# Gated linear recurrence and a cosine-gated MLP on one core: another written-out order of the same steps, with 65 in place of 78 changes of form on TensorE

## The chip, the cores and the metric

The kernel runs on one core of a Trainium2 chip. The metric is the device time of one execution in microseconds, the median of three runs. TensorE (PE in the profile; its weight loads are PEld), VectorE (DVE), ScalarE (ACT), GpSimd (POOL) and the DMA queues, which SyncE (SP) and GpSimd issue, each work through their own instructions in the order in which the kernel emits them.

## The reference

Two layers, one behind the other, in f32. The first is a recurrence over 768 steps for 4 batches and 8 heads of size 48, with a decay per step and channel:

```
state = alpha[:, :, t, :, None] * state + k[t] (outer) v[t]
y[t]  = q[t] @ state
```

The second takes x, the outputs of all heads side by side (3072 tokens x 384), through an MLP with 2048 hidden channels:

```
h = x @ w_in
g = h * cos(h)
out = g @ w_out
```

## The kernel before

Time is cut into pairs J = 0 to 11: three for each batch, each of 256 steps, which are two chunks of 128 in time. In a load, a partition holds two neighbouring steps (e = 0, 1), and the 128 partitions are two halves (c = 0, 1). The recurrence is done with cumulated logarithms, so that all of it is products:

- `load` (SP): alpha ("a"), k, q and v of a pair, 384 KB each. `w1` and `w2` (POOL): the MLP's weights, cast on the way. The load of alpha of pair 3 waits for the last product of yT of pair 1 (GATES, L99); all later loads stand behind it on SP.
- `ln` (ACT) takes logarithms; `mula` (POOL, pairs 3 and up) first multiplies the two steps of a partition. `cums0` and `cums` (PE) sum the logarithms over time by a product with a triangle, and over a chunk by a product with `inchunk`; `sub` (DVE) gives the sums for e = 0 of pairs 3 and up.
- `icp` and `exps` (ACT): exp of the sums, with minus and plus; `eb` is a session of both for a pair, with `ln` of the next. Exp and Sin need different tables, so ACT loads a table (L137, L366) where it goes from one to the other.
- `sk`, `sq` (POOL or DVE): k and q times these; `castv` (POOL): v to bf16; `vpe` and `vev` (PE and ACT or DVE), or `vst` (SP, DMAs), put v of a chunk in another layout. `decay` (POOL): the decay of a chunk.
- `trans` (PE, L259) turns k and q; `evT` (ACT or DVE, L265) takes them to SBUF. `scores` (PE, L273): q k for each chunk c, `mask` (DVE, L278) makes it causal. `outer` (PE, L290): k v of a chunk; `add` (DVE) and `state` (POOL) carry the state from chunk to chunk.
- `yT` (PE, L339): state by q plus scores by v, 32 columns of the array at a time; `evy` (ACT or DVE, L350): to the MLP's input `xT`.
- `m1` u.J (PE, L360): a quarter u of the hidden channels, 12 products; `sin` (ACT, L366), `gate` (DVE, L371); `m2` c p.J (PE, L389 and, for the very last half, L383): part p of the second product for chunk c, 4 products; `evo` (ACT or DVE, L401, L397) and `out` (SP): the result to HBM.
- `idle` n (PE, L415): n products of zeros, 128x512, into a PSUM tile that nobody reads.

Products are full where they use 128 rows and 128 columns of the array: L156, L168, L360, L389, L383, L415. They are partial with 64 rows (L259, L273, L290), with 64 rows and 64 columns (L235), and with 32 columns (L339).

PSUM: tag "h" has three slots of two banks, which `cums0`, `trans`, `scores`, `outer`, `yT` and `m1` share in the order of their emission; tags "x" and "o" have one bank each (`cums` and `vpe`; `m2` and `idle`). A step that takes a slot waits for the last reader of what was in it.

The order is written out: PLAN gives each step of each pair a number, and a letter where the engine is chosen (A for ACT, D for DVE); IDLE gives the products of zeros. The steps are emitted in the order of these numbers, and each engine's queue follows from that. No scheduler moves anything:

```
with tc.manual_schedule():
    for _, _, kind, args in sorted(order, key=lambda x: x[:2]):
        steps[kind](*args)
```

Of the kernel before, what the change touches and what calls it, by code (L numbers as in the profile page):

```python
# [16 lines left out]
def kernel(  # L17
# [11 lines left out]
    B, H, S, D = q.shape  # L29
# [64 lines left out]
    w1 = [consts.tile([C, KT, DF // 2], BF, tag=f"w1{r}", name="w1") for r in range(2)]  # L94
    w2 = consts.tile([C, NF, DM], BF, tag="w2", name="w2")
# [315 lines left out]
    def idle(n):  # L411
# [134 lines left out]
```

## Time and profile before

| what | value |
|---|---|
| time, median of 3 runs | 183.84 us (183.51 to 183.93) |
| profiled execution: span from the first to the last instruction | 182.3 us |
| PE busy | 175.4 us, 96% of the span, 2467 products |
| PEld / DVE / ACT / POOL busy | 132.6 / 134.8 / 129.9 / 71.4 us |
| DMA | 29.47 MB, 162 GB/s in the mean |
| `m2` products (L389) | 368, 67.1 us busy |
| `m1` products (L360) | 576, 67.0 us busy |
| products of zeros (L415) | 38 in the records, 11.1 us busy |

The span covers the program's own instructions; the time of a run has some start and end around it, 1.5 us here. Busy time of PE overlaps between products, since one starts before the one ahead of it has left the array: the time from one start to the next is what a product costs in a row of them. DMA queues are read by when the first user of a load goes on.

### The profile page before, as it was taken

The page shows a single profiled execution, that of the slowest core. Times are in us where ns is not written, and L with a number is a line of the kernel's source. Part 1 is how long each engine was busy: PE and PEld are TensorE (multiplying, and loading weights), DVE is VectorE, ACT ScalarE, POOL GpSimd, SP SyncE. Part 2 cuts the span into 40 slices and gives each one's busy share as a digit, 9 for nine tenths or more (in the row PEclk, how much of TensorE's full clock was granted, in tenths as well). Part 3 has the DMA queues.
Part 4 walks back from the last instruction along what each step waited for, and adds up shares of the span by engine and source line. Part 5 has one row for each costly group of instructions (what it writes and reads, how often), then busy time and mean ns, then how long its engine had stood idle before and what let it go on. Part 6 is the DMA issues. An engine that isn't in the chain of part 4 may idle for free.

```text
span 182.3 us, 5756 instructions
## 1 busy us (share of the span) xinstructions
PE 175.4 (96%) x2467; PEld 132.6 (73%) x2470; DVE 134.8 (74%) x183; ACT 129.9 (71%) x169; POOL 71.4 (39%) x104
## 2 busy tenths in 40 slices
PE   7999899989999999998999999999999999999993
PEld 2455789746697877975799669686876796787872
DVE  7188878678879897599889886978688778363460
ACT  2837687998989999959578999838964174383331
POOL 5145830377777103734894298240720320100000
PEclk9999999999999999999999999999999999999999
DMA  5999999999989959996629905690052142010032
GB/s 148 261 261 220 199 215 221 273 260 265 248 184 283 249 132 295 289 277 202 147 63 229 273 18 166 155 233 0 4 110 83 45 109 81 4 43 4 0 129 86
DMA packets 57801, 29.47 MB, mean 162 GB/s; under 512 B 50992, under 2 KB 56496, under 8 KB 57776
## 3 DMA queue, kind: packets, MB, share of 16 engines
q1 hardware_dynamic: 56256, 25.86, 58.3%
q0 software_dynamic: 1376, 3.15, 9.3%
q8 instruction: 19, 0.31, 0.7%
q10 hardware_dynamic: 144, 0.10, 0.2%
q14 instruction: 6, 0.05, 0.1%
HBM read 25.17 MB, written 4.72 MB: 164 GB/s over the span
## 4 chain that ended last, share of the span: by engine, by line
PE 77%; ACT 11%; DVE 6%; DMA 2%; issue 2%; ACTq 0%
PE h_ps L360 29%; PE o_ps L389 28%; PE y_ps L339 5%; DVE gsb L371 5%; PE idle_ps L415 4%; ACT c_sb L366 3%; PE A_ps L273 3%; PE T_ps L259 3%; DMA a<-in_alpha_dram 2%; PE U_ps L290 2%; ACT L366 2%; PE o_last L383 1%; ACT L137 1%; ACT lna L142 1%; PE cums_h L156 1%
## 5 line engine op out<-in xcount | busy, mean ns | idle before, releaser
L371 DVE TENSOR_TENSOR gsb<-h_ps,c_sb 128x1024 bf16<-128x1024 f32 x48 | 58.2, 1222 | 20.8 <-ACT c_sb L366 19.4
L366 ACT ACTIVATE c_sb<-h_ps,halfpi 128x1024 bf16<-128x1024 f32 x48 | 53.3, 1115 | 26.7 <-PE h_ps L360 26.4
L389 PE MATMUL o_ps<-w,gsb 128*128 128x384 bf16 x368 | 67.1, 327 | 0.6 <-DVE o_sb L401 0.6
L360 PE MATMUL h_ps<-xT,w 128*128 128x256 bf16 x576 | 67.0, 273 | 0.3 <-issue 0.2
L360 PEld LDWEIGHTS <-w 128*128 128x128 bf16 x576 | 62.4, 114 | 2.5 <-DMA w<-in_moe_w_in_dram 0.3
L389 PEld LDWEIGHTS <-gsb 128*128 128x128 bf16 x368 | 33.9, 98 | 21.4 <-issue 1.1
L312 POOL TENSOR_TENSOR un<-us,c 128x384 bf16<-128x384 f32 x20 | 16.8, 838 | 46.2 <-DVE us L304 36.9
L278 DVE TENSOR_TENSOR A_sb<-A_ps,msk 128x1024 bf16<-128x1024 f32 x24 | 28.9, 1216 | 3.4 <-PE A_ps L273 3.4
L217 POOL TENSOR_TENSOR qh<-q,cp 128x384 bf16<-128x384 f32 x13 | 13.8, 1063 | 13.3 <-ACT cp L201 12.2
L213 POOL TENSOR_TENSOR kh<-k,icp 128x384 bf16<-128x384 f32 x15 | 14.9, 1007 | 2.4 <-ACT icp L193 1.0
L220 POOL CAST vp<-v 128x768 bf16<-128x768 f32 x12 | 9.9, 827 | 12.0 <-DMA v<-in_v_dram 12.0
L150 POOL TENSOR_TENSOR a<-a 128x384 f32<-128x384 f32 x9 | 9.0, 1003 | 10.1 <-DMA a<-in_alpha_dram 10.1
L142 ACT ACTIVATE lna<-a 128x768 bf16<-128x768 f32 x12 | 10.1, 844 | 3.5 <-DMA a<-in_alpha_dram 3.3
L415 PE MATMUL idle_ps<-zeros 128*128 128x512 bf16 x38 | 11.1, 439 | 1.4 <-DVE halfpi L77 1.2
L401 ACT COPY o_sb<-o_ps 128x384 f32<-128x384 f32 x13 | 6.2, 478 | 8.5 <-PE o_ps L389 8.5
L137 ACT ACT_TABLE_LOAD x9 | 11.5, 1283 | 0.9 <-PEq L530 0.7
L366 ACT ACT_TABLE_LOAD x9 | 11.5, 1283 | 0.2
L304 DVE TENSOR_TENSOR us<-U_ps,un 128x384 f32<-128x384 f32 x16 | 8.8, 551 | 3.8 <-POOL un L312 2.1
L265 ACT COPY qkT<-T_ps 128x1024 bf16<-128x1024 bf16 x10 | 9.8, 1016 | 1.9 <-PE T_ps L259 1.8
L217 DVE TENSOR_TENSOR qh<-q,cp 128x384 bf16<-128x384 f32 x11 | 6.8, 629 | 5.4 <-DMA q<-in_q_dram 5.3
L265 DVE COPY qkT<-T_ps 128x1024 bf16<-128x1024 bf16 x14 | 9.4, 680 | 1.2 <-PE T_ps L259 1.2
L273 PE MATMUL A_ps<-qkT 48*128 48x128 bf16 x192 | 9.0, 217 | 0.7 <-DVE gsb L371 0.5
(70 smaller groups left out, 156.6 us busy)
## 6 DMA issues: line engine op xcount, KB each, us to landing
a<-in_alpha_dram SPq DMA_DIRECT2D x12, 384.0 KB, 5.9
q<-in_q_dram SPq DMA_DIRECT2D x12, 384.0 KB, 6.1
k<-in_k_dram SPq DMA_DIRECT2D x12, 384.0 KB, 6.0
v<-in_v_dram SPq DMA_DIRECT2D x12, 384.0 KB, 6.3
out_dram<-o_sb SPq DMA_DIRECT2D x23, 192.0 KB, 3.5
vs<-vp SPq DMA_DIRECT2D x36, 64.0 KB, 2.8
w<-in_moe_w_in_dram POOLq DMA_DIRECT2D x2, 768.0 KB, 9.6
w<-in_moe_w_out_dram POOLq DMA_DIRECT2D x4, 384.0 KB, 8.7
```

The costliest lines, as they stand in the source:

```text
L137: nc.scalar.preload_act_table_set("natural_log_exp_and_others")
L213: eng.tensor_tensor(out=kh_t[J % NQ][:, e, :, 0:D], in0=kqv["k", J][:, :, e], in1=icp_, op=ALU.mult)
L217: eng.tensor_tensor(out=qh_t[J % NQ][:, e, :, 0:D], in0=kqv["q", J][:, :, e], in1=cp, op=ALU.mult)
L265: copy(out=qkT_sb[J][:, c], in_=T_ps[J][:, c].rearrange("r n e s -> r n (e s)"))
L273: nc.tensor.matmul(A_ps[J, c][:, a, p, :], qkT[r, c, NP + p, :], qkT[r, c, p, :], start=True, stop=True)
L278: nc.vector.tensor_tensor(out=A_sb[J][:, c].rearrange("s a p t -> s (a p) t"), in0=A_ps.pop((J, c)).rearrange("s a p t -> s (a p) t"), in1 ...
L312: nc.gpsimd.tensor_tensor(out=u, in0=U_sum.pop(n), in1=c2_sb[J][:, :, c].unsqueeze(3).to_broadcast([C, NP, 2, D]), op=ALU.mult)
L360: nc.tensor.matmul(h_ps[J, u][:, f, :], cols, xT[J][:, kk, :], start=(kk == 0), stop=(kk == KT - 1))
L366: nc.scalar.activation(out=c_sb[J, u], in_=h_ps[J, u], func=AF.Sin, bias=halfpi, scale=1.0)
L371: nc.vector.tensor_tensor(out=gsb[J][:, u * FW : (u + 1) * FW], in0=h_ps.pop((J, u)), in1=c_sb.pop((J, u)), op=ALU.mult)
L389: nc.tensor.matmul(o_ps[J, c][:, 0:DM], gsb[J][:, ft, c * C : (c + 1) * C], w2[:, ft], start=(ft == 0), stop=(ft == NF - 1))
L415: nc.tensor.matmul(idle_ps[0], zeros[:, 0:C], zeros, start=True, stop=True)
```

## The change

The numbers in PLAN and IDLE are others; nothing else is edited, and every step of the computation is still done once. The new numbers only count up, in tens, where the old ones looked like nanoseconds; only their order has a meaning in both. What becomes different:

- the order of steps on every engine and on the queues of SP and POOL, from the first load on (alpha of pair 2, then 0 and 1, in place of 0 and 1);
- which of ACT, DVE and POOL does some of the steps: ACT has 10 `evy` in place of 14, 9 `evT` in place of 10, 4 `vev` in place of 5, 15 `evo` of a whole tile in place of 13; DVE has the others; DVE has 8 `sk` and 13 `sq` in place of 9 and 11, POOL the others;
- ACT changes its table 16 times in place of 18;
- on PE, neighbouring products have another form 65 times in place of 78;
- 30 products of zeros in place of 41.

The core of the diff:

```
     PLAN = {
-        "load a": "750 2205 4425 24496 25066 37693 43693 45193 55293 56793 62293 70470",
...
-        "cums0": "5565 7065 13604 - - - - - - - - -",
-        "cums": "5885 11199 13924 36668 44122 49975 61282 73275 86251 91443 105424 117024",
...
-        "icp 1": "8805 11929 15424 - - - - - - - - -",
...
-        "trans": "10624 16461 40648 44533 57020 68793 81884 90868 108663 115899 126133 137709",
-        "evT 0": "11929 17161:A 42626:A 45233:A 60041 70290:A 83189 93123 109551 117529:A 130540:A 139589",
-        "evT 1": "11324 18286 41348 46163:A 58511 71220:A 82584 91568 110631 116599:A 131821 138409:A",
...
-        "mask 0": "16671 19211 46257 47397 69298 74270 86411 102140 116819 126133 144562 152310",
...
-        "m1 1": "20895 30767 50275 64218 73575 93061 91743 120688 129985 146523 158739 168897",
...
+        "load a": "20 70 10 1150 1240 1670 1970 2060 2740 3160 2320 4240",
...
+        "cums0": "60 120 110 - - - - - - - - -",
+        "cums": "130 400 250 1440 1780 2040 2530 2940 3380 3790 4530 4830",
...
+        "icp 1": "230 420 810 - - - - - - - - -",
...
+        "trans": "410 600 1330 1680 2300 2710 3260 3760 4370 4610 5130 5910",
+        "evT 0": "490:A 730:A 1430 1740:A 2410 2780 3300 3830 4400:A 4620 5230 5940:A",
+        "evT 1": "470 670:A 1420 1720:A 2340 2890:A 3310 3780 4460 4630:A 5250 6000",
...
+        "mask 0": "640 860 1650 1840 2730 3270 3480 4220 4660 4760 5760 6120",
...
+        "m1 1": "840 1280 1930 2490 2950 3810 3860 4800 5540 5850 6200 6410",
...
     }
-    IDLE = [(1201, 9), (6413, 2), (7383, 14), (11727, 1), (12377, 4), (15372, 5), (16939, 5), (20459, 1)]
+    IDLE = [(50, 21), (80, 1), (180, 2), (210, 1), (270, 1), (650, 3), (970, 1)]
```

The new order of PE's queue up to the first MLP product (step, then pair):

```
idle x21 | cums0.0 | idle x1 | cums0.2 | cums0.1 | cums.0 | idle x3 | cums.2 | idle x1 | vpe 1.0 | cums.1 | trans.0 |
vpe 0.0 | scores 1.0 | scores 0.0 | outer.0 | trans.1 | idle x3 | vpe 1.1 | scores 1.1 | yT.0 | vpe 0.1 | scores 0.1 |
outer.1 | m1 1.0
```

and the old one:

```
idle x9 | cums0.0 | cums.0 | idle x2 | cums0.1 | idle x14 | trans.0 | cums.1 | idle x1 | scores 1.0 | idle x4 | vpe 0.0 |
cums0.2 | cums.2 | scores 0.0 | outer.0 | vpe 1.0 | idle x5 | trans.1 | idle x5 | yT.0 | scores 0.1 | scores 1.1 |
vpe 1.1 | outer.1 | vpe 0.1 | idle x1 | m1 1.0
```

The new order of ACT up to there is: ln of pairs 0, 2, 1; exps 0.0, exps 0.2, exps 1.0, icp 0.0, icp 1.0, icp 0.2, exps 0.1, exps 1.2, icp 0.1, icp 1.1, evT 0.0, exps 1.1, vev 0.0, evT 1.1, vev 1.1, evT 0.1, evy 0.0, icp 1.2, vev 0.1, sin 1.0.

114 rows, old and new, of the table PLAN are left out of this document.

## The prediction, made before the changed kernel ran

> **What bounds the kernel now.** I read the busy time of each engine in stretches of the span first:
>
> ```profile
> 0.00:21.30 21.30, 18.93 (x254) 9.88 (x258) 14.05 (x42) 12.40 (x23) 10.45 (x29) 1.00 1.08 218
> 21.30:40.00 18.70, 17.89 (x193) 14.91 (x193) 13.59 (x16) 15.34 (x16) 6.74 (x8) 1.00 1.12 238
> 40.00:80.00 40.00, 39.99 (x633) 31.10 (x631) 33.52 (x42) 37.29 (x52) 21.87 (x27) 1.00 1.04 245
> 80.00:120.00 40.00, 39.36 (x633) 29.95 (x631) 34.42 (x43) 33.21 (x43) 22.87 (x28) 1.00 0.65 169
> 120.00:160.00 40.00, 40.00 (x563) 31.16 (x558) 29.75 (x34) 21.88 (x27) 9.46 (x13) 1.00 0.24 65
> ```
>
> Columns: length, then busy time of PE, PEld, DVE, ACT, POOL. From 21.30 us, where the first MLP product starts, to 160 TensorE is idle for 0.81 + 0.01 + 0.64 = 1.46 us: from there on the time is TensorE's own work. ACT is close behind from 40 to 80 (37.3 of 40). The first stretch looks as busy, but 11.1 us in it are products of zeros (L415): there the time is set by loads and by the chain of small steps through ACT, DVE and PE. So the kernel is a lead-in of 21.3 us and a body that runs at the speed of PE, to 179.24 by the chain of waits (last o_last 177.91 + 1.33); the store adds 3.1.
>
> The rows in order of time, for the price of one change between full and partial products (start us, busy us):
>
> ```profile
> 46.54 0.40 PE L273 MATMUL A_ps<-qkT 48*128 48x128 bf16 x8
> 46.87 0.82 PE L389 MATMUL o_ps<-w,gsb 128*128 128x384 bf16 x4
> 47.62 0.52 PE L339 MATMUL y_ps<-qkT,un 128*32 128x128 bf16 x24
> 47.97 0.62 PE L339 MATMUL y_ps<-A_sb,vs 128*32 128x128 bf16 x32
> 48.52 0.40 PE L273 MATMUL A_ps<-qkT 48*128 48x128 bf16 x8
> 48.75 0.51 PE L290 MATMUL U_ps<-vp,kh 64*128 64x96 bf16 x16
> 49.19 0.82 PE L389 MATMUL o_ps<-w,gsb 128*128 128x384 bf16 x4
> 49.85 0.33 PE L156 MATMUL cums<-lna,tri 128*128 128x384 bf16 x1
> ```
>
> Four o_ps take 0.66 from start to start when a full product follows (49.19 to 49.85), 0.75 when a partial one does (46.87 to 47.62). Eight A_ps take 0.23 before U_ps, which has the same 64-row form, and 0.33 before a full product. So a change costs 0.10 us, either way.
>
> Rows of the lead-in:
>
> ```profile
> 4.69 0.84 ACT L142 ACTIVATE lna<-a 128x768 bf16<-128x768 f32 x1 [2.67 <-DMA a<-in_alpha_dram]
> 6.20 0.84 ACT L142 ACTIVATE lna<-a 128x768 bf16<-128x768 f32 x1 [0.66 <-DMA a<-in_alpha_dram]
> 6.95 0.47 ACT L201 ACTIVATE cp<-cums_h 128x384 f32<-128x384 f32 x1
> 9.28 1.26 DVE L213 TENSOR_TENSOR kh<-k,icp 128x384 bf16<-128x384 f32 x2 [0.94 <-DMA k<-in_k_dram]
> 12.25 0.82 POOL L220 CAST vp<-v 128x768 bf16<-128x768 f32 x1 [2.60 <-DMA v<-in_v_dram]
> 13.02 1.72 POOL L125 DMA_DIRECT2D w<-in_moe_w_in_dram  x2
> 21.30 2.88 PE L360 MATMUL h_ps<-xT,w 128*128 128x256 bf16 x24 [0.16 <-issue]
> 34.23 1.00 POOL L150 TENSOR_TENSOR a<-a 128x384 f32<-128x384 f32 x1 [9.19 <-DMA a<-in_alpha_dram]
> ```
>
> Loads 1, 2, 4 and 6 of SP's queue are used at 4.69, 6.20, 9.28 and 12.25: they land one after another, 1.5 us each.
>
> **The change, part by part.** The order of instructions of both kernels, engine by engine, gives the counts.
>
> *Changes of form:* 78 become 65; before the first MLP product (m1 1 of pair 0) 17 become 12, after it 61 become 53. Those ahead of it are not on the bound. After it: 8 x 0.10 = **-0.8 us**.
>
> *Products of zeros:* all 41 stood ahead of the first MLP product; now 29 do, and one stands behind yT of pair 0/1: **+0.2** (0.216 each at full clock). The first 21 stand ahead of the first sums. The rows show 9 of them from 1.19 at 0.43 each, and 0.216 from about 6.1 on, so 21 end at about 1.2 + 11.5 x 0.43 + 9.5 x 0.216 = 8.1.
>
> *The lead-in:* SP loads alpha 2, 0, 1, then k, v, q of pair 0 (before: alpha 0, 1, q, k of pair 0). By the 1.5 us grid alpha 0 lands at 6.2, alpha 1 at 7.7, k 9.2, v 10.7, q 12.2. Walked along the new order with the durations of the rows (ln 0.84, exps/icp 0.37 from start to start, kh on POOL 1.0, evT 0.69 on DVE and 1.02 on ACT, mask 1.21, add 0.55, sums of a chunk 0.53, T_ps 0.57, hops 0.05 to 0.15):
> - ln of pair 1 ends 8.54; sums of pairs 0, 2, 1 and the chunk sums of pair 0 follow the zeros in PE's queue and end at 9.8; the first exps starts at 10.1 (before: 6.95). ACT then does eight of pairs 0, 2 and 1 to the end of icp 0 of pair 1, 13.6; cums of pair 1 waits for that one and stands ahead of trans 0 in PE's queue. **trans 0 at 14.3** (before 10.53).
> - evT 15.64, the second evT, on ACT behind it, 16.7; scores; mask 1 18.4; outer; add 19.5; mask 0 20.7. trans 1 takes the PSUM slot (tag h, three slots) that mask 0 frees: **20.8** (before 16.64). A third slot is held by the sums of pair 2 until icp 1 of pair 2, which ACT has behind evy.
> - evT, vev, evT on ACT to 24.0; yT 24.05 to 24.85; evy 25.4; icp 1 of pair 2 25.85; outer of pair 1 to 26.25. **m1 at 26.2 against 21.30: +4.9.** Ends: 25.0 with no hops and short queue steps on ACT, 27.0 with all of them long.
> - On POOL w_in is issued after cast_v and a kh at 13.1, as before (13.02), so the weights come when they came. w_out is issued behind state 0 of pair 1, from 28.6 (before 18.44); at the 8.7 us to landing of its row the first of it is there at 37.3, and its product at 38.3: hidden with about 1 us. Alpha of pair 3 waits for yT of pair 1 (about 30.2, before 25.14) and lands behind w_out at 40 to 41.4; with mula and ln 1.85 that is 41.8 to 43.3 for cums 3, where PE arrives at 42.15: 0 to 1.2, I take **0.4**.
>
> *The body:* its PE work is 179.24 - 21.30 - 1.46 of waits - 0.8 + 0.2 = 155.9. With no wait at all PE would end at 26.2 + 155.9 = 182.1, 2.9 later than before.
>
> *Waits of the body:* before 1.46. ACT loses 5.5 us of work (two table loads of 1.28, 4 evy, an evT and a vev net of 2 evo), DVE gains 3; neither is on the bound by itself. Places where the new order lets PE wait, by the same walk: yT of pair 1 for add 1 and m1 for gates at 29 to 37, 0.5; the 0.4 above; 61 to 85, scores and m1 behind evT, evy and two ACT sessions (one session from 101.67 to 106.71 in the rows is 5.0 with both table loads), 0.5 to 2.2, I take 1.1, nearer to what the old order shows there; mask, sk and the tail, 0.3. Sum **2.3**, ends 0.5 (what one burst of m1 costs) and 4.5 (each at its long end).
>
> Sum: 26.2 + 155.9 + 2.3 = 184.4 for PE's end against 179.24, **+5.2 us**. The profiled span of 182.3 lies 1.5 below the median of 183.84, so the span comes to 187.5 and the time to **189.0 us**.
>
> **Rivals.**
> 1. *The body has almost no waits.* The order is smooth behind the lead-in. For: fewer ACT steps. Against: the old order has 1.46 itself. 26.2 + 155.9 + 0.5 = 182.6: +3.4 at most, and with m1 at 25.0 +2.2: **186.0 to 187.2**.
> 2. *The granted clock falls in the lead-in.* Products of zeros took 0.43 us at the start and 0.216 later. From trans 0 to m1 PE now works 5 of 12 us, in waits of 1 to 2 us each. If the clock halves there, 2 us of small steps on the chain take 2 more, and the first m1s run double until it is back, about 2 more: **192 to 193**. [...]
> 3. *v of pair 1 is caught by the weights.* Load 9 lands at 16.7 while w_in starts to flow at about 15. The row at 34.23 shows alpha taking 9 us from its issue at 25.14 with weights in flight, against 3.9 for the first load. If v came at 24 instead of 17, vpe 1 would hold PE to 25 in place of 22.1: +3 on the forecast, **192**. Against: in the old order load 9 met w_in at the same time, and came. [...]
> 4. *The other side: the lead-in is no longer than before.* If ACT's exps and the slot of pair 2 did not hold the chain, m1 would start when w_in lands, near 21.3, and 155.9 + 1.5 of waits gives 183.84 - 0.6 = **183.2**. It decides at a start of m1 before 21.9 with the old waits, or before 23.3 with none. Against: every link above is a wait in the built order.
>
> **How the numbers follow.** Forecast 0.62 (own range 187.2 to 191.2), rival 1 0.14, rival 2 0.08, rival 3 0.07, rival 4 0.09. The range leaves out rivals 2 and 4: **185.5 to 192.0**. A difference under 0.2% is about what a measurement of this kernel can't tell from none; rival 4 splits into 0.07 faster and 0.02 the same: faster 0.07, same 0.02, slower 0.91.
>
> **What would show it.** First exps near 10, trans 0 near 14.3, trans 1 near 20.8, first h_ps near 26; four o_ps ahead of a partial product still 0.75; from there PE busy but for 1 to 4 us. Wrong if the first h_ps starts before 24, if the granted clock shows a 5 in the first 30 us, or if the body waits over 5 us.

## The result: 197.8 us in place of 183.9, with the profile after

The changed kernel takes 197.77 us in the median (196.12 to 198.43) against 183.88 (183.51 to 184.15) of the kernel before beside it, a ratio of 1.0747 [1.0694, 1.0800]. The prediction was 189.0 with a range of 185.5 to 192.0: the sign was right, and 8.8 us are missing. The profiled execution took 198.4 us, its span 196.6. In the table below, medians are over all executions, while ratios leave out executions in the slower state, which are one of e3_old9's nine (the profiled one, 186.82 us) and one of e10_lead's four (193.94 us).

The busy time of each engine in stretches of the span (length, PE, PEld, DVE, ACT, POOL, the granted clock of PE, the share of the DMA engines, GB/s), after:

```profile
0.00:30.00 30.00, 21.97 (x245) 11.99 (x245) 14.32 (x40) 13.53 (x24) 11.19 (x29) 0.73 1.01 211
30.00:50.00 20.00, 19.57 (x240) 15.67 (x237) 14.95 (x18) 13.20 (x14) 11.32 (x14) 0.89 0.83 168
50.00:80.00 30.00, 29.17 (x492) 22.02 (x491) 25.44 (x32) 26.12 (x38) 18.79 (x22) 1.00 1.04 248
80.00:120.00 40.00, 38.83 (x542) 30.95 (x541) 34.02 (x40) 31.51 (x41) 20.03 (x24) 1.00 0.77 192
120.00:160.00 40.00, 39.02 (x555) 30.48 (x554) 33.25 (x41) 25.97 (x32) 9.34 (x14) 1.00 0.27 76
```

The row of the granted clock on the page, in 40 slices of 4.9 us, after:

```profile
PEclk9995555999999999999999999999999999999999
```

The lead-in in order of time, PE and the first exps of ACT, after:

```profile
10.60 1.26 ACT L201 ACTIVATE cp<-cums_h 128x384 f32<-128x384 f32 x3 [2.25 <-PE cums_h L168]
14.21 0.80 PE L156 MATMUL cums_h<-lna,tri 128*128 128x384 bf16 x2 [1.51 <-ACT icp L193]
15.14 0.61 PE L259 MATMUL T_ps<-ident_bf,kh 64*128 64x64 bf16 x16
18.00 1.04 PE L273 MATMUL A_ps<-qkT 48*128 48x128 bf16 x16 [1.37 <-ACT qkT L265]
19.93 0.83 PE L290 MATMUL U_ps<-vp,kh 64*128 64x96 bf16 x16 [0.89 <-DVE A_sb L278]
22.54 0.61 PE L259 MATMUL T_ps<-ident_bf,kh 64*128 64x64 bf16 x16 [1.78 <-DVE A_sb L278]
26.91 0.51 PE L339 MATMUL y_ps<-qkT,un 128*32 128x128 bf16 x12 [0.94 <-ACT qkT L265]
30.08 4.24 PE L360 MATMUL h_ps<-xT,w 128*128 128x256 bf16 x19
```

Two things are seen at once. The first h_ps starts at 30.08 instead of 21.30, and the links ahead of it are the forecast's: ACT's exps late, cums of pair 1 behind icp, trans of pair 1 behind the mask that holds its slot. And the clock is at half from 14.06 to 34.54: sixteen T_ps take 0.61 here and 0.41 in the old order. From 50 to 160 us PE is idle for 0.83 + 1.17 + 0.98 = 2.98 of 110, at full clock, where the old order was idle for 0.65 from 40 to 160.

Where the time went, by start times of PE's products (before; after; and the first experiment, the same order at full clock):

| | before | after | after at full clock |
|---|---|---|---|
| first h_ps | 21.30 | 30.08 | 26.07 |
| first o_ps | 29.18 | 44.05 | 38.21 |
| start of PE's last product | 178.98 | 193.24 | 189.21 |
| from the first h_ps to there | 157.68 | 163.16 | 163.14 |

So the 14.26 us in the traces are 4.77 of longer lead-in at full clock, 4.03 of clock, and 5.46 in the body. These are single traces, after's of one of its longer executions (198.40) and the other of one of its shorter ones (194.37): by the medians, 197.77 and 194.61, the clock is 3.2 us.

### The profile page after: what moved, and what is told of

Read it like the earlier page. It is cut to its first block, busy times and chain, and to the rows that moved or that the text cites. A ratio compares the mean times of both kernels' runs of the same rounds, so it can differ in the third digit from the quotient of the medians.

```text
span 196.6 us, 5723 instructions
## 1 busy us (share of the span) xinstructions
PE 181.4 (92%) x2459; PEld 136.7 (70%) x2459; DVE 140.3 (71%) x188; ACT 124.8 (63%) x163; POOL 72.5 (37%) x103
## 4 chain that ended last, share of the span: by engine, by line
PE 54%; DVE 19%; ACT 15%; DMA 6%; issue 3%; SPq 1%; POOL 1%
PE h_ps L360 20%; PE o_ps L389 18%; DVE gsb L371 6%; DMA a<-in_alpha_dram 5%; PE idle_ps L415 5%; DVE A_sb L278 4%; ACT qkT L265 3%; ACT c_sb L366 3%; PE y_ps L339 2%; PE T_ps L259 2%; PE A_ps L273 2%; ACT L366 2%; ACT cp L201 2%; PE U_ps L290 2%; DVE qkT L265 2%
## 5 line engine op out<-in xcount | busy, mean ns | idle before, releaser
L371 DVE TENSOR_TENSOR gsb<-h_ps,c_sb 128x1024 bf16<-128x1024 f32 x48 | 57.8, 1220 | 20.5 <-ACT c_sb L366 19.8
L360 PE MATMUL h_ps<-xT,w 128*128 128x256 bf16 x576 | 69.7, 278 | 1.5 <-DVE gsb L371 1.1
L366 ACT ACTIVATE c_sb<-h_ps,halfpi 128x1024 bf16<-128x1024 f32 x48 | 53.0, 1115 | 22.8 <-PE h_ps L360 22.6
L360 PEld LDWEIGHTS <-w 128*128 128x128 bf16 x576 | 63.3, 115 | 6.0 <-issue 1.5
L213 POOL TENSOR_TENSOR kh<-k,icp 128x384 bf16<-128x384 f32 x16 | 16.8, 1049 | 10.0 <-ACT icp L193 9.6
L265 ACT COPY qkT<-T_ps 128x1024 bf16<-128x1024 bf16 x9 | 9.0, 1015 | 10.2 <-PE T_ps L259 6.7
L220 POOL CAST vp<-v 128x768 bf16<-128x768 f32 x12 | 10.8, 907 | 7.4 <-DMA v<-in_v_dram 7.4
L217 POOL TENSOR_TENSOR qh<-q,cp 128x384 bf16<-128x384 f32 x11 | 11.3, 1031 | 5.7 <-PE T_ps L259 5.7
L213 DVE TENSOR_TENSOR kh<-k,icp 128x384 bf16<-128x384 f32 x8 | 7.8, 972 | 7.7 <-ACT icp L193 7.7
L401 ACT COPY o_sb<-o_ps 128x384 f32<-128x384 f32 x15 | 7.2, 478 | 9.6 <-PE o_ps L389 9.6
L350 DVE CAST xT<-y_ps 128x384 bf16<-128x384 f32 x14 | 8.1, 585 | 4.3 <-PE y_ps L339 2.6
L273 PEld LDWEIGHTS <-qkT 48*128 48x128 bf16 x192 | 6.3, 100 | 6.2 <-issue 4.6
## 6 DMA issues: line engine op xcount, KB each, us to landing
out_dram<-o_sb SPq DMA_DIRECT2D x23, 192.0 KB, 3.1
```

Of the source, the lines that this page charges most:

```text
L213: eng.tensor_tensor(out=kh_t[J % NQ][:, e, :, 0:D], in0=kqv["k", J][:, :, e], in1=icp_, op=ALU.mult)
L217: eng.tensor_tensor(out=qh_t[J % NQ][:, e, :, 0:D], in0=kqv["q", J][:, :, e], in1=cp, op=ALU.mult)
L220: nc.gpsimd.tensor_copy(out=vp_t[J % NV][:, :, :, 0:D].rearrange("s e h d -> s h e d"), in_=kqv.pop(("v", J)))
L265: copy(out=qkT_sb[J][:, c], in_=T_ps[J][:, c].rearrange("r n e s -> r n (e s)"))
L273: nc.tensor.matmul(A_ps[J, c][:, a, p, :], qkT[r, c, NP + p, :], qkT[r, c, p, :], start=True, stop=True)
L360: nc.tensor.matmul(h_ps[J, u][:, f, :], cols, xT[J][:, kk, :], start=(kk == 0), stop=(kk == KT - 1))
```

## The experiments

All have the same steps, but for x1_sin_new and x2_sin_old, which leave out three quarters of the cosines. "Waits" are PE's: what lies between two starts beyond the pitch of the row (0.109 us for an h_ps, 0.1625 for an o_ps, 0.057 for a partial one, 0.096 more at a change of form), in gaps over 0.03 us; counted from the first h_ps to the first product of m1 for pair 2, and from there to the end. A product at half clock counts with what it takes beyond that pitch, so a stretch at half clock (after, e3_old9, h1_oldlead, e7_lead, e11_pair2, e12_mend, e13_pool) is in these columns too.

| kernel | median us | ratio, interval | first h_ps | PE's last start | waits to m1 of pair 2 | behind it |
|---|---|---|---|---|---|---|
| before | 183.88 | | 21.30 | 178.98 | 1.5 | 1.0 |
| after | 197.77 | 1.0747 [1.0694, 1.0800] | 30.08 | 193.24 | 4.2 | 4.5 |
| e1_zeros | 194.61 | 1.0579 [1.0550, 1.0608] | 26.07 | 189.21 | 4.3 | 4.4 |
| e2_old30 | 184.67 | 1.0037 [1.0011, 1.0063] | 22.69 | 180.13 | 1.6 | 0.8 |
| e3_old9 | 185.33 | 1.0052 [1.0016, 1.0089] | 22.63 | 181.66 | 3.6 | 0.4 |
| h1_oldlead | 194.69 | 1.0570 [1.0541, 1.0599] | 23.25 | 189.60 | 7.0 | 4.6 |
| h3_newlead | 188.69 | 1.0259 [1.0218, 1.0301] | 26.41 | 183.52 | 1.7 | 0.4 |
| e4_pair2 | 193.68 | 1.0531 [1.0499, 1.0564] | 25.43 | 188.03 | 3.8 | 4.5 |
| e7_lead | 194.66 | 1.0568 [1.0539, 1.0597] | 25.59 | 189.87 | 5.3 | 4.6 |
| e11_pair2 | 192.30 | 1.0453 [1.0424, 1.0482] | 23.68 | 187.06 | 4.4 | 4.6 |
| e10_lead | 190.35 | 1.0353 [1.0331, 1.0376] | 23.04 | 185.13 | 3.0 | 4.6 |
| e5_wout | 193.14 | 1.0501 [1.0480, 1.0522] | 26.70 | 187.92 | 2.3 | 4.6 |
| e12_mend | 195.87 | 1.0655 [1.0618, 1.0693] | 23.02 | 190.69 | 8.1 | 4.6 |
| e6_spread | 193.75 | 1.0535 [1.0515, 1.0554] | 25.94 | 188.88 | 3.4 | 5.0 |
| e8_letters | 194.31 | 1.0564 [1.0544, 1.0584] | 25.78 | 189.32 | 3.7 | 5.2 |
| x1_sin_new | 191.53 | 1.0418 [1.0399, 1.0438] | 26.02 | 186.44 | 2.9 | 2.9 |
| x2_sin_old | 183.02 | 0.9960 [0.9946, 0.9974] | 21.48 | 177.77 | 1.3 | 0.0 |
| e13_pool | 194.88 | 1.0583 [1.0535, 1.0631] | 26.46 | 189.91 | 2.6 | 6.4 |
| e14_pool | 191.86 | 1.0414 [1.0373, 1.0455] | 25.82 | 186.71 | 3.0 | 3.2 |
| b1_old | 183.47 | 0.9982 [0.9971, 0.9993] | 21.20 | 178.55 | 2.0 | 0.3 |

### The clock

The changed order with 26 more products of zeros in the waits of its lead-in:

```
- cums.2 | idle x1 | vpe 1.0 | cums.1 | trans.0 | vpe 0.0 | scores 1.0 | scores 0.0 | outer.0 | trans.1 | idle x3 | vpe 1.1 | scores 1.1 | yT.0
+ cums.2 | idle x1 | vpe 1.0 | idle x5 | cums.1 | trans.0 | vpe 0.0 | idle x6 | scores 1.0 | scores 0.0 | idle x4 | outer.0 | idle x7 | trans.1 | idle x3 | vpe 1.1 | scores 1.1 | idle x4 | yT.0
```

> The changed kernel with 26 more products of zeros, put where its PE queue waits in the lead-in: 5 ahead of cums of pair 1, 6 ahead of scores 1 of pair 0, 4 ahead of outer of pair 0, 7 ahead of trans of pair 1, 4 ahead of yT of pair 0. Clock theory: the granted clock fell to half from 14.1 to 34.5 us because TensorE had too little to do there; with the zeros it stays full, the first h_ps starts at 26 to 27 us in place of 30.1, its products take 109 ns in place of 213, and the time is 190.5 to 192.5. Rival, the chain theory: the links through ACT and DVE alone set the lead-in, zeros only stand in the way: first h_ps at 30 or later and 197 to 200.

Measured: 194.61, the clock at full speed from 5.85 us to the end of PE's work, first h_ps at 26.07:

```profile
14.13 0.41 PE L259 MATMUL T_ps<-ident_bf,kh 64*128 64x64 bf16 x16
20.62 0.41 PE L259 MATMUL T_ps<-ident_bf,kh 64*128 64x64 bf16 x16 [0.17 <-DVE A_sb L278]
26.07 2.81 PE L360 MATMUL h_ps<-xT,w 128*128 128x256 bf16 x24
```

The clock is shown as a cause. It costs 4.0 us between these two traces and 3.2 by the medians, all of it in the lead-in: the body is as long as after's to 0.02. (After's first 22 h_ps run at 0.213 each, but the 2.3 us that they lose are spent waiting in the other kernel.) Not all of the 4.0 is the fall. The clock first comes to full speed at 7.23 us in after's trace and at 5.85 in this one, so the 21 zeros end 0.7 apart, before anything has fallen. In the seven other traces with this lead-in and its zeros, all at full clock there, the first h_ps starts between 25.78, where full speed comes at 4.01 (e8_letters), and 26.70, where it comes at 7.13 (e5_wout). Against that last one the fall costs 3.4. The time stayed above what was expected, so the body was the larger unknown.

The old order, with 14 zeros ahead of trans 0 cut to 3, and with all but the first 9 taken out:

```
- cums0.1 | idle x14 | trans.0
+ cums0.1 | idle x3 | trans.0
```

> The kernel before, its order untouched, with the 14 zeros ahead of trans of pair 0 cut to 3: 30 zeros in all, as many as the changed kernel has. [...] If the granted clock stays full the time is 183.5 to 184.2; if it falls, 186 to 189. Rival: 11 zeros fewer are 11 x 0.216 us less work, 181.5 to 183.

```
- IDLE = [(1201, 9), (6413, 2), (7383, 14), (11727, 1), (12377, 4), (15372, 5), (16939, 5), (20459, 1)]
+ IDLE = [(20, 9)]
```

> The kernel before, its order untouched, with the first 9 zeros alone. Clock theory: the granted clock falls to half in the lead-in and comes back after a window full of h_ps; small steps on the chain take 2 to 3 us more and about 20 h_ps 0.1 us more each: 187 to 190. Rival: zeros only fill waits, the time is 183.5 to 184.2.

184.67 and 185.33: in the traces the clock did fall, at 11.94 to 15.35 and at 10.41 to 27.47, but the ratios give a loss of only 0.7 and 1.0 us, less than was expected for a fall. The first kernel tests the clock a second time, without an edit: in five of its ten executions the mean granted clock is 0.991 or less, and these took 184.66 to 185.27; of the other five, four took 183.68 to 184.00, which is the time of the kernel before, and one 185.73. So 11 zeros fewer gained nothing by themselves, and the 3.41 us at half clock (11.94 to 15.35) cost about 1 us here. With either edit the small steps end later, and the first h_ps starts at 22.7 and 22.6 instead of 21.3; w_in, there at 20.9 and 20.8, did not hold it. So the zeros of the old order are worth about 1 us to it, while a fall in the new order's lead-in, over 20.5 us, cost 3 to 4.

### Lead-in and body, one at a time

The old order up to the first h_ps, with its zeros, and the new order of all that is left:

```
- idle x21 | cums0.0 | idle x1 | cums0.2 | cums0.1 | cums.0 | idle x3 | cums.2
+ idle x9 | cums0.0 | cums.0 | idle x2 | cums0.1 | idle x14 | trans.0 | cums.1
...
  m1 1.0 | m1 0.0 | yT.1 | idle x1 | m1 3.0
```

> Everything that the old order emits ahead of the first MLP product, in the old order with its zeros, and then the new order for all the rest. First h_ps at 21.3 under a full clock. By the prediction's price of the body (2.3 us of waits against 1.46, 8 changes of form fewer, -0.8) 183.5 to 184.5. By the waits that the changed kernel's trace shows in its body (about 4 us more than the old one) 186 to 188.

194.69, above both ranges. The first h_ps came late, at 23.25, by w_in alone (there at 23.20; the new order issues k, q and v of pair 2 on SP at 11.8 to 15 us, beside w_in, and the old one issues nothing on SP between 10.34 and 25.14), and the body then lost 7.0 us before m1 of pair 2: v of pair 2, issued with the weights in flight, landed at 35.35, cast_v waited 10.44 for it, trans 2.5 for that, and the clock fell at 39.17. Even here the old lead-in bought nothing: the body's price was still open.

The other way round, the new lead-in with the zeros, and the old order of the rest:

```
- m1 1.0 | m1 0.0 | yT.1 | idle x1 | m1 3.0 | m1 2.0 | m1 3.1 | m1 2.1
+ m1 1.0 | m1 0.0 | yT.1 | m1 3.0 | m1 2.0 | m1 0.1 | m2 0 0.0 | m1 2.1
```

> The new order with the zeros in its waits up to the first h_ps, and the old order of everything that is left from there on (queues of SP and POOL too). Theory (lead-in and body add up): first h_ps at 26.1 as in the other kernel with this lead-in, PE's end 157.7 later, 183.7, and a time of 188.3 to 189.0, which is what the prediction gave the whole change (189.0). Rival: the old body fitted only the old lead-in: alpha of pair 3 waits for yT of pair 1 (about 29) and w_out is issued earlier against it, so that cums 3, which the old order puts at 15.7 us behind the first h_ps, waits 1 us or more: 189.5 to 191.

188.69, as the sum says: 4.8 over before for a first h_ps that is 5.1 later, and a body of 157.1. So the new order of the body costs 194.61 - 188.69 = 5.9 us by itself, and lead-in and body add up.

### What makes the lead-in longer

Pair 2's load, ln, sums, exps, icp and decay behind those of pairs 0 and 1:

```
- load a.2 | load a.0 | load a.1 | load k.0
+ load a.0 | load a.1 | load k.0 | load a.2
...
- ln.0 | ln.2 | ln.1 | exps 0.0 | exps 0.2 | exps 1.0 | icp 0.0 | icp 1.0 | icp 0.2
+ ln.0 | ln.1 | exps 0.0 | exps 1.0 | icp 0.0 | icp 1.0 | exps 0.1 | icp 0.1 | icp 1.1 | ln.2
```

> The changed order with the products of zeros in its waits (194.61 us, first h_ps at 26.07), and with pair 2's part of the lead-in (load of alpha, ln, sums, exps, icp, decay) put behind that of pairs 0 and 1, about where the old order has it; 12 of the first 21 zeros go behind the sums of pair 1. The number of zeros ahead of the first h_ps is otherwise kept. Theory: pair 2 in front is what made the lead-in longer (first exps at 10.1 in place of 6.95). Then the first h_ps starts when w_in is there, 22.9 in the run with zeros, so 23.0 to 23.5, and the time is 191.5 to 192.3. Rival: it is the shorter row of slots and evT, vev, evT on ACT between trans 0 and yT; then the first h_ps stays at 25.0 or later and the time at 193.5 or more.

and with pair 0's links as of old on top of that:

```
- vpe 1.0 | idle x5 | cums.1 | trans.0 | vpe 0.0 | idle x6 | scores 1.0
+ trans.0 | cums.1 | scores 1.0 | vpe 1.0 | idle x5 | vpe 0.0 | idle x6
...
- castv.0 (POOL) | sk 1.0 (POOL)
+ sk 1.0 (DVE) | castv.0 (POOL)
```

> The kernel with pair 2 put behind in the lead-in (193.68 us, first h_ps at 25.43, trans 0 at 13.38), and with the links of pair 0 as the old order has them: loads alpha 0, alpha 1, q, k, alpha 2, v; sk of pair 0 wholly on DVE (the new order gives the second half to POOL, where it stands behind castv and its wait for v); trans 0, cums 1, scores 1 of pair 0 ahead of vpe in PE's queue; evT of pair 0 wholly on DVE. Theory: of the 4.8 us of the longer lead-in only 0.6 were pair 2, and the rest is this chain of pair 0. Then trans 0 starts at 10.6 to 11.0, the first h_ps when w_in is there, at 22.5 to 23.5, and the time is 191.0 to 192.0. Rival: it is pair 1's slots and ACT's evT, vev, evT of pair 1; then trans 0 is early, but the first h_ps stays at 24.5 or later and the time above 192.7.

First h_ps at 25.43 and 25.59: on their face, both theories fell. The second trace showed why the runs were no test: trans 0 started at 10.74 as forecast, and trans 1 at 20.41, right behind seven products of zeros. The zeros that filled waits in one order were work on the path in the next. With fewer of them (11 and 15 between trans 0 and the first h_ps):

> The kernel with pair 2 alone put behind in the lead-in (193.68 us, first h_ps at 25.43), with 11 in place of 24 products of zeros between trans 0 and the first h_ps, so that these hold nothing. If pair 2 in front is the cause, the first h_ps comes at 23.0 to 24.0 and the time is 191.5 to 192.6; if pair 0's chain is (sk on POOL behind castv, evT on ACT, trans behind vpe and cums 1), trans 0 stays at 13.4, the first h_ps at 24.8 to 25.4 and the time at 193.0 to 193.7.

> The lead-in with pair 2 behind and pair 0's links as in the old order (194.66 us, first h_ps at 25.59, where trans 1 stood behind 24 products of zeros and started at 20.41), now with 15 of them in place of 29 between trans 0 and the first h_ps. Theory: the longer lead-in is pair 2 in front and pair 0's chain; then trans 1 starts at 16.7 to 17.8 and the first h_ps at 22.5 to 23.6, when w_in is there, and the time is 191.0 to 192.2 (194.61 for the new lead-in with full clock, less 2.5 to 3.5). Rival: ACT's evT, vev, evT of pair 1 and its slots; then trans 1 is early, but the first h_ps stays at 24.5 or later and the time at 193 or more.

192.30 and 190.35. Pair 2 in front is 2.4 us of the lead-in (26.07 to 23.68). With pair 0's chain undone too, yT of pair 0 starts at 20.09 in place of 23.78 and outer of pair 1 ends at 21.84 (20.87 in the old order); the first h_ps then waits for w_in:

```profile
23.04 2.81 PE L360 MATMUL h_ps<-xT,w 128*128 128x256 bf16 x24 [1.20 <-DMA w<-in_moe_w_in_dram]
```

So w_in is the third term: its first half lands at 22.99 here and at 20.98 in the old order, issued at 12.71 and 13.02. The traces give a reason. From 17 to 24 us the weights' queue moves 701 packets alone in the old order, and 632 beside 572 of SP's here. It is not a full one: in e4_pair2 and e11_pair2, with as many loads on SP and w_in issued at 12.3, that half landed at 21.3. In e7_lead and e11_pair2 the clock was at half for 3.41 us (44.73 to 48.14 and 43.13 to 46.54), so their medians hold that too; the starts of the first h_ps lie ahead of it.

### Two queues, and one edit with two results

The four loads of w_out moved up in POOL's queue:

```
- decay.1 | state 0.1 | w2.2 | sk 0.2 | w2.0 | w2.1 | sk 1.2 | castv.2 | w2.3 | state 1.1
+ decay.1 | w2.2 | w2.0 | w2.1 | w2.3 | state 0.1 | sk 0.2 | sk 1.2 | castv.2 | state 1.1
```

> The changed order with the products of zeros in its waits (194.61 us), and with the four loads of w_out issued by POOL behind the last decay of pair 1 (about 22 us) in place of behind state 0 of pair 1 (28.3 to 32.8). Theory: the waits of PE at 40 to 45 us are the two queues' work, 1.3 us for w_out itself and 1.1 us for alpha of pair 3, which lands at 42.5 because it shares the DMA engines with w_out. Then w_out is there at 29 to 36, alpha of pair 3 at 36 to 38, both waits go, and the time is 192.0 to 192.6. Rival: the loads of q and v of pair 2, which landed at 27.9 and 29.2, are now caught by w_out and land at 33 or later; cast_v and trans of pair 2 come late and the time stays within 0.7 of 194.6 or rises.

In the kernel that this starts from (the changed order at full clock), PE waits at 40 to 45 us:

```profile
40.39 1.46 PE L389 MATMUL o_ps<-w,gsb 128*128 128x384 bf16 x8 [0.18 <-DMA w<-in_moe_w_out_dram]
42.76 0.81 PE L389 MATMUL o_ps<-w,gsb 128*128 128x384 bf16 x4 [0.91 <-DMA w<-in_moe_w_out_dram]
44.49 0.32 PE L156 MATMUL cums<-lna,tri 128*128 128x384 bf16 x1 [0.92 <-ACT lna L142]
```

Issued at 28.3 to 32.8, w_out landed at 33.2 to 42.7, and alpha of pair 3 at 42.5. With the edit all three waits are gone, the body is 1.9 shorter, the time 1.5: 193.14. The theory held, a little below its price. The rival was half right too: v of pair 2 did come late, POOL's cast of it started at 36.90 in place of 32.02, but PE reached pair 2 only at 39.8 and had to wait 0.3 in all.

The same edit on the mended lead-in:

> The mended lead-in (190.35 us, first h_ps at 23.04) with w_out issued early as in the other run (behind the last decay of pair 1). If the causes add up, the 0.95 us wait for alpha of pair 3 at 39 goes, the first h_ps stays at 23.0, PE's end falls from 185.1 to 184.0 to 184.3 and the time to 189.1 to 189.6; what is left over the old order, 5.3 to 5.8 us, is 1.7 us of later first h_ps and 3.6 to 4.0 us of waits in the body. If w_out now shares the engines with w_in's second half, which the product at 27 already waits 0.66 us for, the time stays within 0.4 of 190.35.

195.87, 5.5 us worse than without it. POOL's cast of v of pair 2, first in the mended lead-in and then with w_out moved up as well:

```profile
29.25 0.82 POOL L220 CAST vp<-v 128x768 bf16<-128x768 f32 x1 [0.85 <-DMA v<-in_v_dram]
```

```profile
37.10 0.82 POOL L220 CAST vp<-v 128x768 bf16<-128x768 f32 x1 [10.47 <-DMA v<-in_v_dram]
37.98 0.35 PE L235 MATMUL vs_ps<-vp,ident_bf 64*64 64x384 bf16 x2 [1.75 <-POOL vp L220]
40.68 0.61 PE L259 MATMUL T_ps<-ident_bf,qh 64*128 64x64 bf16 x16 [2.01 <-POOL qh L217]
```

and the DMA queues of the second kernel from 26 to 33 us (packets, MB, share of 16 engines; q0 carries the weights, q1 SP's loads):

```profile
q0 software_dynamic: 473, 1.29, 93.7%
q1 hardware_dynamic: 471, 0.17, 14.3%
```

In these 7 us the two queues moved nearly the same number of packets, 473 and 471 (616 and 614 from 19 to 26 us), but 1.29 MB and 0.17, which is 2.7 KB a packet for the weights and 0.36 for SP's loads. v comes at 37 in both kernels with this edit, where w_out joins w_in at 21 to 23 us. In the longer lead-in that was hidden; here PE is 3.7 us earlier and comes to pair 2 at 36.2. It waited 1.8 and 2.0, and from 39.43, within the second wait, to 46.26 the clock was at half, which cost about 2 us more (twelve o_ps at 0.320 in place of 0.1625).

### What makes the body wait

The column on the right of the table is the plain finding: whatever the lead-in and the queues did, the new order waits 4.4 to 4.6 us behind m1 of pair 2, and the old one 0.4 to 1.0. Four theories were tried, on the kernel with w_out early. The chain that ended last, by engine, before and in that kernel, points to the queues of the others: DVE's share is 20% in place of 6, ACT's 17 in place of 11.

```profile
PE 77%; ACT 11%; DVE 6%; DMA 2%; issue 2%; ACTq 0%
```

```profile
PE 57%; DVE 20%; ACT 17%; issue 3%; POOL 0%; POOLq 0%
```

First, full products moved ahead of a product that waits:

```
- m1 0.4 | m1 3.4 | m1 2.4 | m2 0 0.3
+ m1 0.4 | m2 0 0.3 | m1 3.4 | m1 2.4
...
- m1 0.5 | m1 2.5 | m1 0.6 | m1 3.5 | m2 1 0.4
+ m1 0.5 | m2 1 0.4 | m1 2.5 | m1 0.6 | m1 3.5
...
- m2 1 0.6 | m1 3.7 | m2 1 1.6
+ m2 1 0.6 | m2 1 1.6 | m1 3.7
...
- scores 1.10 | m1 0.9 | m1 0.8 | m1 2.8 | m2 1 0.7
+ scores 1.10 | m2 1 0.7 | m1 0.9 | m1 0.8 | m1 2.8
...
- yT.10 | scores 0.11 | scores 1.11 | m2 0 0.9
+ yT.10 | m2 0 0.9 | scores 0.11 | scores 1.11
```

> The kernel with w_out issued early, and five m2 steps moved in PE's queue ahead of a product that waited there: m2 0 0 of pair 3 ahead of m1 3 of pair 4 (with evo 1 of pair 2 on DVE in place of ACT), m2 1 0 of pair 4 ahead of m1 2 of pair 5, m2 1 1 of pair 6 ahead of m1 3 of pair 7, m2 1 0 of pair 7 ahead of m1 0 of pair 9, m2 0 0 of pair 9 between yT of pair 10 and scores of pair 11 (with evo 1 of pair 8 on DVE). Only the last adds a change of form. The waits there were 0.64, 0.57, 0.34, 0.43 and 0.89 us with the products of zeros in the lead-in. Theory: these waits are local, PE comes to a PSUM slot or to an evT too early, and a product of 0.65 us that is ready covers them: 2.4 us less than the kernel with w_out early alone, so 189.6 to 190.2. Rival: ACT and DVE are behind as a whole in these stretches, and the wait comes back one or two steps later: less than 0.8 us gained.

Waits 5.0 in place of 4.6, the time 0.6 more. Three of the five places lost their wait (0.57 to 0.12, 0.41 and 0.42 to nothing), and it came back at 88 (0.54), 119 (0.66 for 0.47) and 133 (0.72 for 0.34). Of the two moves that also put an evo on DVE, one made o_ps wait 0.93 for that evo, behind gates, and the other gained nothing.

Second, halves of evT and evy that are split over two engines:

```
-        "evT 0": "490:A 770:A 1470 1780:A 2450 2820 3340 3870 4440:A 4660 5270 5980:A",
-        "evT 1": "470 700:A 1460 1760:A 2380 2930:A 3350 3820 4500 4670:A 5290 6040",
+        "evT 0": "490:A 770:A 1470 1780:A 2450 2820 3340 3870 4440 4660 5270 5980",
+        "evT 1": "470 700:A 1460 1760:A 2380 2930 3350 3820 4500 4670 5290 6040",
...
-        "evy 1": "840:D 1060 1870 2410:D 2870:D 3780 3840:D 4730:D 5450:D 5360:D 6130 6280:D",
+        "evy 1": "840:D 1060 1870:D 2410:D 2870:D 3780 3840:D 4730:D 5450 5360:D 6130:D 6280:D",
```

> The kernel with w_out issued early (193.14 us) in which the two halves of evT of pairs 5, 8, 9, 11 and of evy of pairs 2, 4, 9, 10, 11 are both done by DVE, and those of evy of pair 8 both by ACT; in the new order each of these pairs has one half on ACT and one on DVE. The trace shows the second half of such a pair waiting for the first on the other engine (DVE 1.20 for ACT's evT at 159, ACT 2.54 for DVE's evy at 75, with the table load for sin behind it). Theory: a good part of the body's waits comes from these split halves: the waits at 75 to 82, 118, 138 and 159, together 2.6 us, lose 1.2 or more, and the time is 190.5 to 192.0. Rival: the waits are set by ACT's and DVE's work as a whole and by the order of the slots; DVE has more to do now, and the time is within 0.4 of 193.1 or above it.

194.31. The split is real (DVE idles 1.20 for the other half of a tile that ACT is copying), and its wait at 79 went, but with both halves on DVE yT of pair 10 waited 1.58 for a gate, m1 of pair 9 1.25. With more work on DVE these runs can't tell what the split itself costs.

Third, ACT's load: sin for a quarter of each tile, in the new order and in the old.

```
-        c_sb[J, u] = sb.tile([C, FW, T2], BF, tag="c_sb", name="c_sb", bufs=BUF["c"])
-        nc.scalar.activation(out=c_sb[J, u], in_=h_ps[J, u], func=AF.Sin, bias=halfpi, scale=1.0)
+        c_sb[J, u] = sb.tile([C, 1, T2], BF, tag="c_sb", name="c_sb", bufs=BUF["c"])
+        nc.scalar.activation(out=c_sb[J, u], in_=h_ps[J, u][:, 0:1], func=AF.Sin, bias=halfpi, scale=1.0)
...
-        nc.vector.tensor_tensor(out=gsb[J][:, u * FW : (u + 1) * FW], in0=h_ps.pop((J, u)), in1=c_sb.pop((J, u)),
+        nc.vector.tensor_tensor(out=gsb[J][:, u * FW : (u + 1) * FW], in0=h_ps.pop((J, u)), in1=c_sb.pop((J, u)).to_broadcast([C, FW, T2]),
```

> The kernel with w_out issued early (193.14 us; its waits of PE from 53 to 165 us are 4.2), with sin computed for a quarter of each tile only and the gate multiplying all four quarters with that one: this leaves out three quarters of the cosines. A sin takes some 0.4 us in place of 1.11, 34 us less for ACT in all; DVE and PE do what they did. Theory (ACT's load makes the waits): they fall to 1.2 or less, and the time to 189.5 to 190.7. Rival (the order of slots, DVE and the table loads): they stay above 2.8, and the time above 191.7.

> The kernel before with the same edit, sin for a quarter of each tile (three quarters of the cosines are left out), as the control. Its waits of PE from 40 us on are 1.4, of which 0.62 and 0.31 wait for a gate. If ACT's load makes the waits, it gains 0.3 to 1.0, to 182.8 to 183.5, and the two orders then differ by the lead-in (4.7) and w_in's part alone, 5.5 to 6.5 less the fewer changes of form; if not, it gains less than 0.3.

Sins fell from 53.0 to 22.7 us in all. The old order lost its last waits (183.02); the new one went from 4.6 to 2.9, between the two theories. So ACT's load is in part of the waits, but with 30 us less of it most of them stay.

Fourth, DVE's queue: the sk and sq steps that the new order gives to DVE go to POOL, of pairs 6 to 11 and then of 8 to 11 only (the ten steps below; the first run has sq 1 of pairs 6 and 7 and sk 0 of pair 7 besides).

```
- sk 0.8 (DVE) | sk 0.9 (DVE) | sk 0.11 (DVE) | sk 1.11 (DVE) | sq 0.9 (DVE) | sq 0.11 (DVE) | sq 1.8 to sq 1.11 (DVE)
+ sk 0.8 (POOL) | sk 0.9 (POOL) | sk 0.11 (POOL) | sk 1.11 (POOL) | sq 0.9 (POOL) | sq 0.11 (POOL) | sq 1.8 to sq 1.11 (POOL)
```

> The kernel with w_out issued early (193.14 us, 4.6 us of waits behind the first m1 of pair 2) with the thirteen sk and sq steps of pairs 6 to 11 that DVE has in the new order given to POOL, which is busy for 13 of 40 us from 100 to 140. Theory: DVE's queue makes the waits, kh and qh standing ahead of the gates and evT for which PE waits at 95, 101, 118, 128 and 133 (2.0 us together); they lose 1.3 or more, and the time is 191.0 to 191.9. Rival: kh and qh come later from POOL (1.0 to 1.3 each) than from DVE, and trans waits for them instead; the time is 192.7 or more.

194.88: the waits at 101, 118 and 133 were gone, but kh of pair 7 came from POOL so late that its trans waited 2.27, and behind that wait the clock was at half for a while: the 72 h_ps that start at 98.21 took 9.70 us, where 72 at full clock take 8.05 (e12_mend, at 27.53). Without pairs 6 and 7:

> The kernel with w_out issued early (193.14 us), with the ten sk and sq steps of pairs 8 to 11 that DVE has in the new order given to POOL; those of pairs 6 and 7 stay on DVE. With those of 6 and 7 too, the waits at 118 and 133 us (0.47 and 0.34) and the one at 101 (0.57) were gone, but trans of pair 7 waited 2.27 for kh from POOL and the clock fell for one window. Theory (DVE's queue makes them): the waits behind 100 us fall from 3.1 to 1.7 to 2.2 with no new one, and the time to 191.8 to 192.4. Rival: another trans waits for POOL, and the time stays at 192.8 or more.

191.86, as expected. PE's waits from 100 to 134 us, with w_out early, and then with the sk and sq of pairs 8 to 11 on POOL:

```profile
101.05 4.09 PE L360 MATMUL h_ps<-xT,w 128*128 128x256 bf16 x36 [0.40 <-DVE gsb L371]
118.48 0.41 PE L259 MATMUL T_ps<-ident_bf,kh 64*128 64x64 bf16 x16 [0.31 <-DVE kh L213]
128.49 1.50 PE L360 MATMUL h_ps<-xT,w 128*128 128x256 bf16 x12 [0.25 <-DVE gsb L371]
132.81 0.41 PE L259 MATMUL T_ps<-ident_bf,kh 64*128 64x64 bf16 x16 [0.20 <-DVE gsb L371]
```

```profile
127.77 1.50 PE L360 MATMUL h_ps<-xT,w 128*128 128x256 bf16 x12 [0.35 <-DVE gsb L371]
```

So 1.4 of the 4.6 us are DVE's queue of pairs 8 to 11, kh and qh standing ahead of the gates and evT that PE needs. No run has this edit and the lighter ACT together; taken place by place from the two traces, one or the other removes 2.5 of the 4.6. Of the 2.1 left, 1.6 are at 75, 138 and 159 us, where the second half of a split tile ends last. No edit took those away without a new wait, so that the split costs this is argued from the trace, not shown.

### The old order, mended with the same idea

```
- sq 0.6 (DVE)
+ sq 0.6 (POOL)
...
- trans.9 | scores 0.8 | outer.8 | cums.11 | m2 1 0.6 | m2 1 1.6 | scores 1.8 | outer.9
+ trans.9 | scores 0.8 | cums.11 | m2 1 0.6 | m2 1 1.6 | outer.8 | scores 1.8 | outer.9
```

> The kernel before with two edits, each against one wait of PE that its trace shows: sq 0 of pair 6 on POOL in place of DVE (at 78.47 it stands ahead of three gates, the last of which holds the slot for which scores 1 of pair 5 waits 0.62 us at 82.4), and outer of pair 8 taken from behind scores 0 of pair 8, where it waits 0.31, to ahead of scores 1 of pair 8. If these waits are local, as the ones of the old order look, the time falls by 0.6 to 0.9, to 182.9 to 183.3. If the waits come back one step later, it stays at 183.6 to 184.2.

183.47, a ratio of 0.9982 [0.9971, 0.9993]: lower by 0.3 us where 0.6 to 0.9 was expected, with an interval that ends just below 1. Both waits went (1.0 to 0.3 behind m1 of pair 2); 0.4 was lost ahead of that, 0.26 of it at 33 us, where an o_ps waited that had not waited before. The cause of that stays open.

## Why the prediction was wrong, by its own steps

- **Changes of form, -0.8, and one product of zeros, +0.2: right.** Body less waits is 155.10 before and 154.43 in the changed order at full clock, -0.67 against -0.6. After shows the same row prices, 0.75 for four o_ps ahead of a partial product and 1.31 for eight ahead of a full one:

```profile
90.95 0.82 PE L389 MATMUL o_ps<-w,gsb 128*128 128x384 bf16 x4
91.70 0.41 PE L259 MATMUL T_ps<-ident_bf,kh 64*128 64x64 bf16 x16
92.61 1.47 PE L389 MATMUL o_ps<-w,gsb 128*128 128x384 bf16 x8
93.92 0.33 PE L156 MATMUL cums<-lna,tri 128*128 128x384 bf16 x1
```

- **The lead-in, +4.9 (m1 at 26.2): right at full clock**, 26.07 (25.78 to 26.70 in the other traces), and its links were the ones named (trans 0 at 14.13, trans 1 at 20.62). The sum for the 21 zeros gives 8.2 and not the 8.1 written; the first sums start at 8.02 in that trace and at 8.70 in after's. "The weights come when they came" was off: w_in was issued as before (12.97) and landed 2 us later. In this lead-in that was hidden; in the mended one it was the bound.
- **Rival 2, the granted clock, 0.08: the first step that failed.** Its price came out right, 4 against 4.03 in the traces and 3.2 by the medians, but by luck: the small steps lost 3.4 and not 2 (the other 0.6 is the later start of full speed in after's trace), and the first h_ps, which did run at half, lost nothing in the sum, since without that they wait for w_out. Its chance was not right: 0.08 was an estimate without a run behind it, since the trace of before has full clock from 6.07 us to the end of PE's work and can't show what brings a fall. In after's trace products streamed for 0.33 of the 3.41 us ahead of it (10.64 to 14.06); with zeros in the waits the clock stayed full (e1_zeros). The zeros in the old order were the hint: they stand exactly where its small steps wait.
- **"Hidden with about 1 us" (w_out): failed as a term.** The piece for the first product was priced, and it came as said (37.44 against 37.3, its product at 38.21), by luck again: the piece that is issued first, at 28.33, landed at 33.15, and the one that the product needs was issued at 29.91 and took 7.5. Those for the second and the fourth came at 40.35 and 42.71, and PE waited 1.3 for them. "I take 0.4" for alpha of pair 3: 1.09, as it landed at 42.5, later than the 40 to 41.4 given, since w_out was still in flight.
- **Rival 3 (v of pair 1 caught by the weights) did not happen:** POOL's cast of it starts at 17.38 at full clock and at 18.38 in after's trace, with no wait for the load.
- **"29 to 37, 0.5" and "61 to 85 ... 1.1": right**, 0.55 and 0.95. The stretch between them was left out: trans of pair 3 and yT of pair 2 waited 1.1 at 48 to 50.
- **"mask, sk and the tail, 0.3": the largest mis-sized term**, 3.4 us from 85 on. The walk stopped at each wait that it could name in the first half of the body and took the second half to be like the old order. But the waits there come from DVE's queue, ACT's sessions and split halves, on which the prediction only counted work ("neither is on the bound by itself") and not order.

Together, in the traces: 4.77 + 4.03 + 5.46 against 4.9 + 0 + 0.2. The sum lacked the clock, 4.0 (3.2 by the medians), which stood among the rivals, and waits of 6.1 in place of 0.8. "The body waits over 5 us" and "a 5 in the first 30 us" were both named as what would make it wrong, and both happened.

## What to carry to other kernels

- A saving that is counted in instructions (here 0.7 us for fewer changes of form) is sure and small; the price of the order that buys it (5.9 us in the body here) lies in the in-order queues of the other engines and must be walked to the end of the kernel, all pieces of a load and all steps of a queue included.
- A wait in a lead-in had two prices here, its own and that of the clock (4.0 us between the traces of after and e1_zeros, 3.2 by the medians). Where zeros stand in an old kernel, ask what they hold up before they are moved; and where they stay, take care that they do not become work on the path when the waits around them shrink.
- An edit that was worth 1.5 us in one order cost 5.5 in another, since the load that it delays was needed 3.7 us sooner there. A mend must be measured in the order in which it will live.

## What the runs showed of the hardware that was not expected

- **The clock fell behind a stretch that was far from idle.** The stretches at half clock last whole multiples of 3.41 us: 20.48 in after's trace (14.06 to 34.54; full speed first came at 7.23, 6.83 ahead of the fall), 3.41 in those of e2_old30, e7_lead and e11_pair2, 17.06 in e3_old9's, 6.83 in e12_mend's. For after and before I worked out from the records for what share of each 3.41 us on this grid products were streaming (columns of a product at 512 per 0.216 us, twice that time at half clock, overlaps counted once). In after's trace the share was 0.33 ahead of the fall (10.64 to 14.06), 0.43 to 0.81 in the five stretches behind which the clock stayed at half (14.06 to 31.12), and 1.00 in the one behind which it came back (31.12 to 34.54). Full speed first came behind a share of 1.00 in after's trace (3.82 to 7.23) and of 0.83 in before's (2.65 to 6.07). The lowest share at full clock with no fall behind it was 0.51 in after's (191.55 to 194.96) and 0.68 in before's (176.73 to 180.15). Where between these numbers the clock changes was not tried.
- **The same kernel fell in some executions and not in others:** e2_old30 in five of ten, with a mean granted clock of 0.991 or less. Where the grid lies differs from trace to trace: with the same 21 zeros in front, full speed first came at 7.23 us (after), 5.85 (e1_zeros), 4.01 (e8_letters) and 7.13 (e5_wout). That this is the reason is a guess; no run shows it.
- **One wait of 2.27 us was followed by a fall** in the midst of full work, in the kernel with sk and sq of pairs 6 to 11 on POOL (e13_pool); in the one with the mended lead-in and w_out early (e12_mend) the clock fell within the second of two, 1.75 and 2.01 us. A wait of 2.18 us was followed by none: in h1_oldlead the 24 h_ps behind it took 2.81 us, as at full clock in e1_zeros.
- **Small packets beside large ones moved few bytes, in as many packets** (e12_mend, 26 to 33 us): 471 packets of SP's against 473 of the weights, 0.17 MB against 1.29.
- **Two halves of one tile on two engines run one after the other** in this program: the second waits for the first, 1.20 us at 159 in e5_wout, though it writes other columns. Whether only the program's waits do this was not tried.
